# Top-k attention and a hard-swish feed-forward on one Trainium2 core: the reciprocals of the softmax move from VectorE to GpSimd, the shifts of exp from GpSimd to ScalarE

## The chip, the cores and the metric

One core of one Trainium2 chip runs the whole program. Its engines have instruction streams of their own and meet at semaphores: TensorE (PE in the profile; its weight loads are PEld), VectorE (DVE), ScalarE (ACT), GpSimd (POOL), and SyncE (SP), which here only issues DMAs. The metric is the device time of one execution in microseconds (us), the median of several runs; lower is better.

## The reference

```python
# q, k, v: (8 batches, 8 heads, 576 tokens, 64); top_k = 32
scores = scale * (q @ k.T)
kth = 32nd largest of each row
scores = where(scores >= kth, scores, -1e9)
scores = scores - max(scores)
attn = exp(scores); attn = attn / (sum(attn) + 1e-9)
x = (attn @ v) as (4608 tokens, 512)
h = x @ w_in                       # (4608, 2048)
g = h * clip(h + 3, 0, 6) / 6
out = g @ w_out                    # (4608, 512)
```

The two weight matrices arrive as float64. The kernel turns them into float32 itself, from the two 32-bit words of each number.

## The kernel before

The unit of attention work is a *duo*: two pairs of heads times one tile of 128 query rows, so four rows of 576 scores on each partition. The 64 tokens left over of each sequence (576 = 4 x 128 + 64) make smaller duos, here called rest duos, with two such rows. There are 64 full and 16 rest duos. For each row VectorE finds the 32 largest scores, by four MAX8 and three MATCH_REPLACE8. One duo is eight *slots*: in a slot VectorE does one MAX8 and one replacement on the two rows of a pair (one row in a rest duo), and every other step of the program is hung on a slot number. `u` is the pair in the duo, 0 or 1.

```python
def convert(dst, src):                     # one of 32 chunks of the weights, 128 x 512
    st = kqpool.tile(...); nc.sync.dma_start(st[:], src)
    yield
    a = gpool.tile(...); y = gpool.tile(...)
    nc.scalar.activation(a[:], hi.bitcast(F32), AF.Abs)
    nc.gpsimd.tensor_scalar(a[:], a[:], HI_MOST, HI_LEAST, ALU.min, ALU.max)
    nc.scalar.activation(y[:], lo, AF.Copy, bias=2.0, scale=2.0**-51)
    yield
    nc.vector.tensor_scalar(au, au, 3, None, ALU.logical_shift_left)              # L117
    nc.vector.scalar_tensor_tensor(out=yu, in0=hi, scalar=0x80000000, in1=yu, ...) # L118
    yield
    nc.gpsimd.tensor_tensor(dst.bitcast(I32), a.., y.., ALU.add)                  # L123

def shift(self, u):                                                # cut to its core
    nc.gpsimd.tensor_tensor(d[:, 0:nt], m[:, 0:nt, TOP_K - 1], m[:, 0:nt, 0], ALU.subtract)  # L263
    nc.gpsimd.tensor_scalar_mul(d[:, 0:nt], d[:, 0:nt], scale)                    # L266

def exp(self, u):
    for t in range(nt):  # row <- Prelu(kth - row): zero point at the 32nd largest   L273
        nc.scalar.activation(row, row, AF.Prelu, bias=m[:, t, TOP_K - 1 : TOP_K], ...)
    for t in range(nt):  # row <- exp(..), and its sum into den                      L278
        nc.scalar.activation(row, row, AF.Exp, bias=self.less[u][:, t : t + 1], ..., accum_out=self.den[:, u, t : t + 1])
    nc.scalar.activation(d, d, AF.Copy, bias=EPS)                                 # L283

def inverse(self, u):
    nc.vector.reciprocal(d, d)                                                    # L287

def weights(self, u):   # GpSimd: row * (1/den), then the float32 split in two halves of 16 bits
    ...                                                                           # L297, L306
def flip(self, u):      # DMA transpose of the 16-bit halves, on SyncE's queue
def join(self, u):      # the halves put together again: u = 0 on ScalarE, u = 1 on GpSimd  L318
def values(self, dst):  # TensorE: attn @ v into PSUM
def place(self):        # ScalarE: PSUM -> x, which queues a block of feed-forward
```

A feed-forward block (128 tokens) is cut into 16 *pieces* of matmul: 8 for `h`, 8 for `acc`. The main loop emits them between the steps of attention:

```python
due += ((left > 0) + (left >= 24) / 8 + (left >= 48) / 8) / (2 if u and u.rest else 1)
piece(int(due))         # left: pieces queued and not emitted
```

The slots of a duo's steps, counted from its own first slot:

```python
usual = dict(shift0=3, exp0=4, inverse0=9, weights0=10, flip0=12, join0=15,
             shift1=7, exp1=8, inverse1=13, weights1=14, flip1=16, join1=19, values=22, place=23)
behind = dict(usual, values=25, place=26)
early = dict(...)       # duos 0 and 1
soon = dict(..., values=16, place=17)   # the last two duos
```

`behind` holds for the duos from 10 to the fifth from the end.

## Time and profile before

| | |
|---|---|
| time, median of 3 runs | 1580.76 us (1580.28 to 1581.73) |
| profiled span | 1578.5 us |
| PE busy | 1456.9 us, 92% |
| DVE busy | 1466.8 us, 93% |
| ACT busy | 1096.3 us, 69% |
| POOL busy | 1144.5 us, 73% |
| mean granted TensorE clock | 0.963 |

Two engines are busy for more than nine tenths of the span, so neither share alone says which of them sets the time. The profile's rows by slice show VectorE at work from the start and idle in the last two of the 40 slices, and TensorE little used in the first five and at work to the end: work moves from the one to the other as the program runs. What matters is how the two are coupled in each stage.

### The profile page before, as it was taken

How to read it: one execution, taken by the hardware profiler on the slowest of the kernel's cores; microseconds unless marked ns; L12 is line 12 of the kernel's file. 1: busy time of each engine (PE TensorE's matmuls, PEld its weight loads, DVE VectorE, ACT ScalarE, POOL GpSimd, SP SyncE). 2: the span in 40 equal slices, each digit the busy share in tenths (PEclk: the TensorE clock that was granted, in tenths of full speed). 3: DMA queues.
4: the chain of work that ended last, by engine and by line, in shares of the span. 5: the costliest groups of instructions: out<-in, count | busy, mean ns of one | idle time of the engine just before them, and what ended most of it. 6: DMA issues, size and time to landing. Idle time of an engine off the chain costs nothing.

```text
span 1578.5 us, 28787 instructions
## 1 busy us (share of the span) xinstructions
PE 1456.9 (92%) x10272; PEld 1039.0 (66%) x10272; DVE 1466.8 (93%) x3105; ACT 1096.3 (69%) x1865; POOL 1144.5 (73%) x1264
## 2 busy tenths in 40 slices
PE   5256799979999999998999999999999999999899
PEld 3153566567767777666777777776777767677675
DVE  6999999999999999999999999999999999999700
ACT  6675777777777777777776786777766787777621
POOL 4868687777867777867687777867687777767841
PEclk9568999989999999999999999999999999999999
DMA  8652543444344543545254543446244443533410
GB/s 236 159 181 45 113 83 81 94 91 97 76 90 89 101 83 76 101 85 119 55 106 76 97 89 82 93 93 116 57 96 87 98 88 74 103 65 68 83 22 14
DMA packets 450319, 144.49 MB, mean 92 GB/s; under 512 B 433280, under 2 KB 441472, under 8 KB 450176
## 3 DMA queue, kind: packets, MB, share of 16 engines
q1 hardware_dynamic: 450176, 142.65, 43.5%
q8 instruction: 81, 1.33, 0.3%
q14 instruction: 62, 0.51, 0.1%
HBM read 45.09 MB, written 9.44 MB: 35 GB/s over the span
## 4 chain that ended last, share of the span: by engine, by line
DVE 51%; PE 35%; POOL 5%; issue 3%; ACT 3%; DMA 1%; SPq 1%; POOLq 0%; ACTq 0%; DVEq 0%
DVE m L250 26%; DVE wk L254 22%; PE h L365 14%; PE acc L385 13%; PE pv L338 4%; PE big L232 3%; POOL e L306 1%; DVE y L118 1%; POOL sc L297 1%; DMA t<-e 1%; POOL eT L318 1%; DVE a L117 1%; PE big L177 1%; ACT sc L278 1%; ACT eT L318 1%
## 5 line engine op out<-in xcount | busy, mean ns | idle before, releaser
L250 DVE MAX8 m<-wk 128x8 f32<-128x576 f32 x864 | 613.1, 746 | 2.2
L385 PE MATMUL acc<-w_out,g 128*128 128x512 f32 x1152 | 516.9, 600 | 14.1 <-POOL g L380 14.1
L365 PE MATMUL h<-xT,w_in 128*128 128x128 f32 x4096 | 485.5, 279 | 17.3 <-ACT xT L348 17.3
L365 PEld LDWEIGHTS h<-xT,w_in 128*128 128x128 f32 x4096 | 475.0, 195 | 39.5 <-issue 18.2
L254 DVE MATCH_REPLACE8 wk<-m,wk 128x576 f32<-128x576 f32 x576 | 423.7, 742 | 0.0
L385 PEld LDWEIGHTS acc<-w_out,g 128*128 128x128 f32 x1152 | 213.6, 191 | 260.4 <-issue 238.6
L297 POOL TENSOR_SCALAR sc<-sc,den 128x576 f32<-128x576 f32 x288 | 213.8, 753 | 229.9 <-DVE den L287 222.7
L306 POOL COPY e<-sc 128x2304 uint16<-128x2304 uint16 (+1 forms) x192 | 320.3, 1678 | 10.2
L278 ACT ACTIVATE sc<-sc,shift 128x576 f32<-128x576 f32 x288 | 220.4, 769 | 40.5 <-POOL shift L266 37.7
L318 ACT COPY eT<-t 128x2304 uint16<-128x2304 uint16 (+1 forms) x82 | 215.9, 2632 | 37.9 <-DMA t<-e 35.3
L273 ACT ACTIVATE sc<-sc,m 128x576 f32<-128x576 f32 x288 | 210.1, 777 | 46.2 <-DVE m L250 46.0
L338 PE MATMUL pv<-eT,vm 128*64 128x128 f32 (+1 forms) x2560 | 164.0, 273 | 57.9 <-ACT eT L318 45.8
L254 DVE MATCH_REPLACE8 wk<-m,sc 128x576 f32<-128x576 f32 x288 | 211.8, 742 | 0.0
L318 POOL COPY eT<-t 128x2304 uint16<-128x2304 uint16 (+1 forms) x78 | 203.8, 2613 | 6.9 <-DMA t<-e 6.5
L338 PEld LDWEIGHTS pv<-eT,vm 128*64 128x64 f32 x2560 | 135.2, 141 | 109.3 <-ACT eT L318 49.7
L250 DVE MAX8 m<-sc 128x8 f32<-128x576 f32 x288 | 203.3, 742 | 2.4 <-ACT sc L236 2.4
L373 ACT ACTIVATE g<-h,three 128x512 f32<-128x512 f32 x144 | 98.5, 684 | 150.0 <-PE h L365 140.6
L380 POOL TENSOR_TENSOR g<-g,hs 128x512 f32<-128x512 f32 x144 | 185.0, 1285 | 12.1 <-POOL g L379 0.2
L233 ACT COPY sc<-big 128x2048 f32<-128x2048 f32 (+1 forms) x65 | 119.3, 1836 | 26.1 <-PE big L232 26.0
L232 PE MATMUL big<-kq 64*128 64x512 f32 x512 | 136.4, 653 | 0.0
L379 POOL TENSOR_SCALAR g<-g 128x512 f32<-128x512 f32 x144 | 89.2, 620 | 62.6 <-ACT g L373 52.4
L395 ACT ACTIVATE o<-acc 128x512 f32<-128x512 f32 x36 | 21.4, 595 | 106.6 <-PE acc L385 106.6
(47 smaller groups left out, 1113.1 us busy)
## 6 DMA issues: line engine op xcount, KB each, us to landing
landed<-in_k_dram SPq DMA_DIRECT2D x64, 128.0 KB, 3.0
landed<-in_q_dram SPq DMA_DIRECT2D x64, 128.0 KB, 3.0
st<-in_moe_w_in_dram SPq DMA_DIRECT2D x16, 512.0 KB, 5.1
vm<-in_v_dram SPq DMA_DIRECT2D x64, 128.0 KB, 2.3
st<-in_moe_w_out_dram SPq DMA_DIRECT2D x16, 512.0 KB, 6.6
out_dram<-o SPq DMA_DIRECT2D x32, 256.0 KB, 2.4
t<-e SPq DMA_TRANSPOSE x160, 4.6
landed<-in_k_dram SPq DMA_DIRECT2D x32, 32.0 KB, 2.8
```

The lines of the kernel that those rows point to most:

```text
L232: nc.tensor.matmul(banks[:, 2 * i + hh, :], pr.qT[d, qs], pr.kT[d, :])
L250: nc.vector.max(self.m[u][:, t, 8 * r : 8 * r + 8], self.cur[t])
L254: nc.vector.match_replace(wk, self.m[u][:, t, 8 * r : 8 * r + 8], self.cur[t], LOWEST)
L273: nc.scalar.activation(row, row, AF.Prelu, bias=m[:, t, TOP_K - 1 : TOP_K], scale=-1.0, alpha=FLAT)
L278: nc.scalar.activation(row, row, AF.Exp, bias=self.less[u][:, t : t + 1], scale=-scale / FLAT, accum_out=self.den[:, u, t : t + 1],)
L297: nc.gpsimd.tensor_scalar(row, row, self.den[:, u, t : t + 1], 1.0, ALU.mult, ALU.mult)
L306: nc.gpsimd.tensor_copy(halves[:, :, to : to + c1 - c0], words)
L318: copy(eT[:, 0 : self.nb, :] .rearrange("p c q -> p (c q)") .bitcast(U16) .rearrange("p (x h) -> p h x", h=2), self.t16[u][:, 0 : 2 * self ...
L338: nc.tensor.matmul(pv[hh * D : (hh + 1) * D, u * w : (u + 1) * w], pr.vm[:, hh, c, :] if c < J else pr.vr[:, hh, :], rhs, start=(c == 0), ...
L365: nc.tensor.matmul(h[:, (f - f0) * P : (f - f0 + 1) * P], w_in[:, i, f * P : (f + 1) * P], xT[:, i, :], start=(i == 0), stop=(i == NHP - 1),)
L380: nc.gpsimd.tensor_tensor(g[:], g[:], hs[:], ALU.mult)
L385: nc.tensor.matmul(acc[:], gs[f // nf][:, f % nf * P : (f % nf + 1) * P], w_out[:, f, :], start=(f == 0), stop=(f == NFC - 1),)
```

## The change

Six things are changed together.

1. The reciprocal of the sums of exp leaves VectorE. GpSimd takes both pairs of a duo at once: x = den^(-1) as a power, then one Newton step x(2 - den x), four small instructions (`inverse`). Adding 1e-9 to the sums (`settle`) stays on ScalarE, once a duo. The first two duos and the last do it pair by pair.
2. The shift of exp leaves GpSimd: ScalarE works out scale x (kth - max) with one Copy and one Identity for each row.
3. For the first 16 of the 32 weight chunks, `y` is written to PSUM and `ys` takes VectorE's result in SBUF. The pool `g` goes from 8 to 7 buffers.
4. The first load of q is issued from ScalarE's queue, beside that of k on SyncE's.
5. Left-over tokens get two buffers in place of one (`xr`), and the rest duos of batch 2 are spread over the batch as in the later ones; in the last batch they come one query tile later.
6. The slots are set anew. From `exp` of pair 1 (slot 8) to `values` it is still 14 slots in `usual`. `soon` (values at 19) now holds for duos 2 to 9 and five near the end, `usual` for 10 to 29, `behind` from 30 to the ninth from the end.

The aim is to free VectorE, which paces the attention, of work that is not the search for the 32 largest.

```diff
--- before.py
+++ after.py
@@ -59,8 +59,8 @@
     wkpool = pool("wk", 1)
     mpool = pool("m", 4)
     xtpool = pool("xt", 3)
-    xrpool = pool("xr", 1)
-    gpool = pool("g", 8)
+    xrpool = pool("xr", 2)
+    gpool = pool("g", 7)
     hpool = pool("h", 2)
     opool = pool("o", 1)
     ps_big = pool("ps_big", 1, space=PSUM)
@@ -74,6 +74,8 @@
     make_identity(nc, ident[:])
     three = const([P, 1], "three")
     nc.vector.memset(three[:], 3.0)
+    minus = const([P, 2, 2], "minus")
+    nc.vector.memset(minus[:], -1.0)
     w_in = const([P, NHP, FF], "w_in")
     w_out = const([P, NFC, DM], "w_out")
@@ -93,7 +95,8 @@
     WC = 512
-    def convert(dst, src):
+    def convert(dst, src, early):
@@ -104,7 +107,11 @@
         words = st[:].rearrange("p (n two) -> p n two", two=2)
         lo, hi = words[:, :, 0], words[:, :, 1]
         a = gpool.tile([P, WC], F32, tag="g", name="a")
-        y = gpool.tile([P, WC], F32, tag="g", name="y")
+        y = (
+            ps_w.tile([P, WC], F32, tag="w", name="yp")
+            if early
+            else gpool.tile([P, WC], F32, tag="g", name="y")
+        )
         nc.scalar.activation(a[:], hi.bitcast(F32), AF.Abs)
         nc.gpsimd.tensor_scalar(a[:], a[:], HI_MOST, HI_LEAST, ALU.min, ALU.max)
@@ -113,15 +120,16 @@
+        ys = gpool.tile([P, WC], F32, tag="g", name="ys") if early else y
         au, yu = a[:].bitcast(U32), y[:].bitcast(U32)
         nc.vector.tensor_scalar(au, au, 3, None, ALU.logical_shift_left)
         nc.vector.scalar_tensor_tensor(
-            out=yu, in0=hi, scalar=0x80000000, in1=yu,
+            out=ys[:].bitcast(U32), in0=hi, scalar=0x80000000, in1=yu,
             op0=ALU.bitwise_and, op1=ALU.bitwise_or,
         )
         yield
         nc.gpsimd.tensor_tensor(
-            dst.bitcast(I32), a[:].bitcast(I32), y[:].bitcast(I32), ALU.add
+            dst.bitcast(I32), a[:].bitcast(I32), ys[:].bitcast(I32), ALU.add
         )
     def weight_chunks():
@@ -143,16 +151,17 @@
             self.b, self.hp = b, hp
             self.vm, self.vr, self.kr = vms[hp], vrs[hp], krs[b % 2 * NHP + hp]
-        def load(self):
+        def load(self, queue=None):
             h0 = 2 * self.hp
             t = self.landed = kqpool.tile([P, 2 * J + 1, 2, D], F32, tag="kq", name="landed")
-            for i, src in enumerate((k, q)):
+            for i, (src, eng) in enumerate(((k, nc.sync), (q, queue or nc.sync))):
                 for hh in range(2):
-                    nc.sync.dma_start(
+                    eng.dma_start(
                         t[:, i * J : (i + 1) * J, hh, :],
                         src[self.b, h0 + hh, 0:JP, :].rearrange("(p j) d -> p j d", j=J),
                     )
-                nc.sync.dma_start(
+                eng.dma_start(
                     t[i * R : (i + 1) * R, 2 * J, :, :],
                     src[self.b, h0 : h0 + 2, JP:S, :].rearrange("h s d -> s h d"),
                 )
@@ -259,11 +268,16 @@
         def shift(self, u):
             nt, m = self.nt, self.m[u]
-            d = self.less[u] = mpool.tile([P, 2], F32, tag="shift", name="shift")
-            nc.gpsimd.tensor_tensor(
-                d[:, 0:nt], m[:, 0:nt, TOP_K - 1], m[:, 0:nt, 0], ALU.subtract
-            )
-            nc.gpsimd.tensor_scalar_mul(d[:, 0:nt], d[:, 0:nt], scale)
+            d = self.less[u] = mpool.tile([P, 2, 2], F32, tag="shift", name="shift")
+            nc.scalar.activation(d[:, 1, 0:nt], m[:, 0:nt, 0], AF.Copy, scale=-scale)
+            for t in range(nt):
+                nc.scalar.activation(
+                    d[:, 0, t : t + 1],
+                    m[:, t, TOP_K - 1 : TOP_K],
+                    AF.Identity,
+                    bias=d[:, 1, t : t + 1],
+                    scale=scale,
+                )
         def exp(self, u):
@@ -276,15 +290,24 @@
             for t in range(nt):
                 row = self.row(u, t)
                 nc.scalar.activation(
-                    row, row, AF.Exp, bias=self.less[u][:, t : t + 1], scale=-scale / FLAT,
+                    row, row, AF.Exp, bias=self.less[u][:, 0, t : t + 1], scale=-scale / FLAT,
                     accum_out=self.den[:, u, t : t + 1],
                 )
-            d = self.den[:, u, 0:nt]
+        def inverse(self, us):
+            n, nt = len(us), self.nt
+            d = self.den[:, us[0] : us[-1] + 1, 0:nt]
+            x = mpool.tile([P, 2, 2], F32, tag="inv", name="inv")[:, 0:n, 0:nt]
+            y = mpool.tile([P, 2, 2], F32, tag="inv2", name="inv2")[:, 0:n, 0:nt]
+            nc.gpsimd.tensor_tensor(x, d, minus[:, 0:n, 0:nt], ALU.pow)
+            nc.gpsimd.tensor_tensor(y, d, x, ALU.mult)
+            nc.gpsimd.tensor_scalar(y, y, -1.0, 2.0, ALU.mult, ALU.add)
+            nc.gpsimd.tensor_tensor(d, x, y, ALU.mult)
+        def settle(self, us):
+            d = self.den[:, us[0] : us[-1] + 1, 0 : self.nt]
             nc.scalar.activation(d, d, AF.Copy, bias=EPS)
-        def inverse(self, u):
-            d = self.den[:, u, 0 : self.nt]
-            nc.vector.reciprocal(d, d)
         def weights(self, u):
@@ -408,9 +431,9 @@
             duos += [Duo(h, qt) for h in halves]
-            if qt == (0 if b == B - 1 else J - 1) and not 2 < b < B - 1:
+            if qt == (1 if b == B - 1 else J - 1) and not 1 < b < B - 1:
                 duos += [Duo(h, J) for h in halves]
-            elif 2 < b < B - 1 and qt % 2 == 0:
+            elif 1 < b < B - 1 and qt % 2 == 0:
                 duos.append(Duo(halves[qt // 2], J))
     assert J == NHP == 4
     per_batch = 2 * J + 2
@@ -418,7 +441,7 @@
     for u in duos[:2]:
         u.early = True
     todo = []
-    blocks = []
+    blocks, rests = [], []
     left = 0
     gates = []
@@ -442,8 +465,7 @@
     def queue(*block):
         nonlocal left
         todo.append(feed_forward(*block))
-        if block[0] is not state.get("xr"):
-            blocks.append(todo[-1])
+        (rests if block[0] is state.get("xr") else blocks).append(todo[-1])
         left += P // 8
     state = {}
@@ -454,7 +476,7 @@
         b, hp = u.pairs[0].b, u.pairs[0].hp
         if u.rest:
             if b % 2 == 0 and hp == 0:
-                while state.get("rest") in todo:
+                while len(rests) > 1 and rests[-2] in todo:
                     piece()
                 state["xr"] = xrpool.tile([P, NHP, P], F32, tag="xr", name="xr")
             u.values(state["xr"][:, hp : hp + 2, (b % 2) * R : (b % 2 + 1) * R])
@@ -478,7 +500,6 @@
                 for i in range(2)
             ]
             queue(state["xr"], rows)
-            state["rest"] = todo[-1]
     chunks = list(weight_chunks())
     landing, converting, adding = [], [], []
@@ -486,7 +507,7 @@
     def land(count=1):
         for _ in range(min(count, len(chunks))):
-            c = convert(*chunks.pop(0))
+            c = convert(*chunks.pop(0), early=len(chunks) >= NFC)
             next(c)
             landing.append(c)
@@ -513,7 +534,7 @@
         return pairs[b + 1][at - first] if b + 1 < B and 0 <= at - first < NHP else None
     first = pairs[0]
-    first[0].load()
+    first[0].load(nc.scalar)
     land(2)
     first[1].load()
     first[0].transpose()
@@ -530,33 +551,49 @@
     usual = dict(
-        shift0=3, exp0=4, inverse0=9, weights0=10, flip0=12, join0=15,
-        shift1=7, exp1=8, inverse1=13, weights1=14, flip1=16, join1=19, values=22, place=23,
+        shift0=3, exp0=4, shift1=7, exp1=8, settle01=8, inverse01=11, weights0=12, weights1=14,
+        flip0=14, flip1=16, join0=17, join1=19, values=22, place=23,
     )
     behind = dict(usual, values=25, place=26)
     early = dict(
-        shift0=3, exp0=3, inverse0=4, weights0=4, flip0=5, join0=8,
-        shift1=7, exp1=7, inverse1=8, weights1=8, flip1=9, join1=12, values=12, place=13,
+        shift0=3, exp0=3, settle0=3, inverse0=4, weights0=4, flip0=5, join0=8,
+        shift1=7, exp1=7, settle1=7, inverse1=8, weights1=8, flip1=9, join1=12, values=12, place=13,
     )
     soon = dict(
-        shift0=3, exp0=3, inverse0=5, weights0=5, flip0=7, join0=10,
-        shift1=7, exp1=7, inverse1=9, weights1=9, flip1=11, join1=14, values=16, place=17,
+        shift0=3, exp0=4, shift1=7, exp1=8, settle01=8, inverse01=9, weights0=9, weights1=11,
+        flip0=11, flip1=13, join0=14, join1=16, values=19, place=20,
+    )
+    last = dict(
+        shift0=3, exp0=3, settle0=3, inverse0=5, weights0=5, flip0=7, join0=10,
+        shift1=7, exp1=7, settle1=7, inverse1=8, weights1=8, flip1=9, join1=11, values=12, place=12,
     )
     queued = {}
     for m in range(ND):
-        for part, at in (early if m < 2 else soon if m >= ND - 2 else behind if per_batch <= m < ND - 4 else usual).items():
+        if m < 2:
+            when = early
+        elif m == ND - 1:
+            when = last
+        elif m < per_batch or m >= ND - 6:
+            when = soon
+        else:
+            when = behind if 3 * per_batch <= m < ND - 8 else usual
+        for part, at in when.items():
             queued.setdefault(8 * m + at, []).append((m, part))
     def parts(slot, late=None):
         for m, part in sorted(queued.get(slot, []), key=lambda x: x[1][:-1] != "shift"):
-            if late is not None and (part[:-1] in ("inverse", "weights")) != late:
+            if late is not None and (part[:7] in ("inverse", "weights")) != late:
                 continue
             if part == "values":
                 values(m)
             elif part == "place":
                 place(m)
+            elif part[:-1] in ("settle0", "inverse0"):
+                getattr(duos[m], part[:-2])((0, 1))
+            elif part[:-1] in ("settle", "inverse"):
+                getattr(duos[m], part[:-1])((int(part[-1]),))
             else:
                 getattr(duos[m], part[:-1])(int(part[-1]))
```

(Lines that are empty are cut.)

## The prediction

> **What bounds the kernel now.** I read the busy shares first, then busy time in stretches cut where the work changes, then VectorE's waits, then single instructions in the timeline. The page's first part:
>
> ```profile
> PE 1456.9 (92%) x10272; PEld 1039.0 (66%) x10272; DVE 1466.8 (93%) x3105; ACT 1096.3 (69%) x1865; POOL 1144.5 (73%) x1264
> ```
>
> Two engines are above nine tenths. The same by stretches (columns: stretch, its length, then busy us and instructions of PE, PEld, DVE, ACT, POOL; then granted clock, DMA share, GB/s); 13.6 is VectorE's first MAX8, 144.1 the first slot of duo 4, 708.6 that of duo 36, 1491.3 the end of the last MAX8:
>
> ```profile
> 708.60:1491.30 782.70, 774.06 (x5659) 556.66 (x5655) 777.35 (x1670) 570.25 (x974) 590.68 (x652) 1.00 0.44 87
> 1491.30:1578.50 87.20, 79.02 (x446) 54.92 (x444) 0.17 (x2) 19.30 (x33) 31.68 (x31) 0.98 0.10 23
> 244.20:708.60 464.40, 450.85 (x3243) 320.65 (x3243) 461.85 (x994) 339.94 (x578) 345.83 (x385) 0.98 0.45 89
> 13.60:144.10 130.50, 63.21 (x318) 43.04 (x318) 126.89 (x229) 89.50 (x148) 95.19 (x96) 0.71 0.54 160
> ```
>
> Up to 144 VectorE works nearly without a gap and TensorE half the time. In the middle both are at 97 to 99%. After 1491 VectorE has nothing left and TensorE needs 87 us for the backlog. So the span is VectorE's run of duos plus TensorE's tail. VectorE's own waits say who paces whom:
>
> ```profile
> DVE a L117 <- POOL a L109: 13.3, 2, 10.0
> DVE den L287 <- ACT den L283: 9.3, 4, 6.7
> DVE m L250 <- ACT sc L236: 2.4, 2, 1.7
> DVE three L76 <- PEq L616: 0.8, 1, 0.8
> ```
>
> 10.0 of the first line is the start and 6.7 of the second comes after the last MAX8, in the tail. Between, VectorE waits some 8 us in all. From the timeline's first MAX8 of each duo, a full duo takes 19.40 us and a rest duo 11.22, every time but two: duo 19 took 12.09 and duo 73 13.45, where a reciprocal waited for the sums. So VectorE is the pacemaker, but TensorE is close behind. I worked out what TensorE must do in one of the middle batches, with back-to-back times from the timeline: a block's 128 `h` records take 14.3 us and its 32 `acc` records 13.75, so one of 16 pieces is 1.75 us, and 4.5 blocks are 126 us; the scores of 8 full duos at 2.46 and 2 rest duos at 2.1 are 24; values, 8 at 2.33 and 2 at an estimated 1.5, are 22; four transposes at 1.15 are 4.5. Sum 176 us, against 8 x 19.40 + 2 x 11.22 = 177.6 of VectorE. TensorE has only 1.6 us a batch to spare.
>
> **What the Trainium skill says.** "SBUF — State Buffer", section "SBUF: two separate sides": VectorE and GpSimd share one pair of ports under an exclusive lock, taken by a VectorE instruction with two SBUF inputs or a two-port mode; the loser blocks. The trace agrees: L118, which reads `hi` and `y` from SBUF, takes 0.68 us free and 1.75 beside a GpSimd instruction. With `y` in PSUM it has one SBUF input. "ScalarE: Activation LUTs", section "What ACT_TABLE_LOAD costs": an ACTIVATE has about 186 ns fixed, 93 more for each per-partition operand, and neighbours overlap by about 93. The trace: the Copy of the sums takes 204 ns, and the instruction behind it starts 0.11 later. No page that I found states what a power costs on GpSimd; that number is missing from my sum.
>
> **The change part by part.**
>
> *The reciprocals.* The groups by shape (busy us, mean ns):
>
> ```profile
> L118 DVE SCALAR_TENSOR_TENSOR y<-st,y 128x512 uint32<-128x512 uint32 x32 | 30.2, 943 | 0.0
> L287 DVE RECIPROCAL den<-den 128x2 f32<-128x2 f32 x128 | 19.7, 154 | 7.2 <-ACT den L283 7.0
> ```
>
> 128 + 32 reciprocals are 24.6 us of busy time, but their busy time isn't what they cost. The timeline of VectorE, in a full and in a rest duo (start, duration):
>
> ```profile
> 187.78 0.73 DVE L254 MATCH_REPLACE8 wk<-m,wk 128x576 f32<-128x576 f32 x1
> 188.44 0.15 DVE L287 RECIPROCAL den<-den 128x2 f32<-128x2 f32 x1
> 188.51 0.73 DVE L250 MAX8 m<-wk 128x8 f32<-128x576 f32 x1
> ```
>
> ```profile
> 400.99 0.76 DVE L250 MAX8 m<-wk 128x8 f32<-128x576 f32 x1
> ...
> 401.86 0.74 DVE L254 MATCH_REPLACE8 wk<-m,wk 128x576 f32<-128x576 f32 x1
> 402.52 0.15 DVE L287 RECIPROCAL den<-den 128x2 f32<-128x2 f32 x1
> 402.64 0.76 DVE L250 MAX8 m<-wk 128x8 f32<-128x576 f32 x1
> ```
>
> From MATCH_REPLACE8 to MAX8 it is 0.73 us in a full duo, and 0.66 where no reciprocal stands between (190.61 to 191.27). So one costs 0.07 us of pace, 0.14 a duo. In a rest duo it is 0.78 with and without (400.21 to 400.99): the MAX8 there has to wait for the row just written, and the reciprocal fills that gap. Gain: 60 full duos after conversion x 0.14 = 8.4, the first four 0.6, and the stalls in duos 19 and 73 (0.87 + 2.23 = 3.1). Together 12.1 us, half of the busy time.
>
> *Conversion.* The first 16 L118 took 16.0 us by the timeline; at 0.68 each they would take 10.9. If PSUM removes the collisions: 5.1 us off VectorE's first 130 us, where nothing else bounds. The last 16 stay.
>
> *The first load.* The transposes of k start at 4.54, those of q at 6.67, after q's load, which SyncE issued from 2.82 on. Issued beside k's from 0.7 on, q should land 1.8 us sooner, and everything to the first MAX8 hangs on it. Gain 1.8.
>
> *Shifts.* GpSimd loses 160 x (0.22 + 0.22) = 69 us and gains 83 inverses of four small instructions: three at 0.22 and a power that I put at 0.3 to 0.6, so 80 to 105 us. GpSimd stays near 74%. ScalarE gains three small ACTIVATEs for a full pair, two for a rest pair: with ends overlapped I put 0.55 and 0.35 us, 128 x 0.55 + 32 x 0.35 = 82 us, and loses 77 of 160 additions (16 us): up 66 us to some 74%. Its waits for GpSimd's shift (37.7 us, 26 times) go. None of this is on VectorE's path, as long as ScalarE's copies of scores come in time.
>
> *Slots.* Stepping through the emission rule, I counted the pieces put out by each duo. The new table puts batch 0's blocks three slots earlier, so TensorE is three pieces ahead up to duo 29, but from duo 36 (224 pieces out in both) to duo 71 both kernels emit the same number at every duo. At the end of VectorE's work 534 of 576 pieces are out before, 535 after: the tail is one piece shorter, 1.75 us. The blocks begin at slot 21 in both. TensorE's wait of 4.4 us for a `join` on GpSimd at 1491, when `values` of duo 77 came due, should shrink, as these last duos now follow `soon`; I count 3.
>
> *Sum.* 12.1 + 5.1 + 1.8 + 1.75 + 3 = 23.8 us. From this I take back: of VectorE's 7.1 us gained after duo 36 (35 full duos x 0.14, and 2.2) TensorE can follow only in part, since it idles 8.6 us there in all and its work of 176 us meets a pace of 176.5 (8 x 19.26 + 2 x 11.22): 3 us go into a longer tail. And 2 us for new stalls: at duos 10, 20, 30, 68 and 74, all right after a rest duo, the scores were copied only 0.4 to 1.9 us before VectorE needed them, and ScalarE gets about 1 us more to do there. Net 19: 1580.8 - 19 = 1562; I predict 1561.
>
> **Rivals.** *TensorE is the bound already.* For it: the chain that ended last runs on TensorE from 733 to 1220, and the busy share is 98.9% after duo 36. Then only what comes before TensorE fills up counts (start and conversion, 7 us), and the time is about 1573. Against it: VectorE's period is 19.40 to a hundredth, so TensorE never held it up, and at 1491 TensorE had caught up and was waiting. *ScalarE or GpSimd takes the place.* If the power takes 3 us in place of 0.5, GpSimd rises by 200 us to over 85%, chains run past their slots, TensorE, which takes its work in order, stops at `values`, and the scores behind it come late: 1590 to 1620. For it: the four rest-duo edges with under 1 us of slack, and the fact that a Newton step is needed at all, which speaks for a coarse and thus perhaps short routine. Against it: GpSimd idles 27%, 222.7 us of it waiting for the very reciprocal it now makes itself. *All of it arrives,* the rest-duo stalls too, and TensorE closes its idle time: 1550.
>
> **Range and chances.** The sure parts (reciprocals in the first half, start, most of conversion) are 10 us, the full sum 24, and the GpSimd rival costs some tens. Range 1547 to 1578. Faster by over 2% means under 1549.1, more than my whole sum before deductions: 0.08. Slower by over 2% (over 1612) needs the slow power: 0.04.
>
> **What would show it.** Full duos at 19.26 between first MAX8s, rest duos still at 11.22; duo 4 begins near 136.5; first MAX8 near 11.8; the first 16 of VectorE's second conversion instruction at 0.7 each; VectorE's last MAX8 near 1472 to 1475 and a tail of 83 to 87 us behind it. I am wrong if the power takes over 1 us, if VectorE waits for scores at many duo edges, or if the tail grows by what VectorE gains.

## The result, and the profile after

The changed kernel takes 1624.13 us (median of 4 runs, 1623.21 to 1625.23), the kernel before 1581.24 in the same session: a ratio of 1.0269, 95% interval 1.0251 to 1.0287. It is slower by 43 us. The prediction, 1561, had the wrong sign.

Busy shares of the changed kernel, first part of its page:

```profile
PE 1470.6 (91%) x10272; PEld 1043.4 (64%) x10272; DVE 1456.2 (90%) x2946; ACT 1161.7 (72%) x2236; POOL 1199.5 (74%) x1276
```

The loads are as the change intends: VectorE 10.6 us less, ScalarE 65.4 more (predicted 66), GpSimd 55 more. TensorE does the same 10272 matmuls in 13.7 us more, at a mean granted clock of 0.955 instead of 0.963. No engine comes near its span but the two that did before. So the 43 us can't be read off the busy shares. The chain of work that ended last shows a different picture from before, when VectorE held 51% and TensorE 35% of it (before, then after):

```profile
DVE 51%; PE 35%; POOL 5%; issue 3%; ACT 3%; DMA 1%; SPq 1%; POOLq 0%; ACTq 0%; DVEq 0%
PE 57%; POOL 15%; DVE 14%; DMA 5%; ACT 4%; issue 3%; SPq 2%; POOLq 0%; ACTq 0%
```

The same by stretches (length, busy us of PE, PEld, DVE, ACT, POOL, then clock, DMA share, GB/s); 13.4 is the first MAX8, 154.5 the first slot of duo 4, 258.0 that of duo 10, 733.2 that of duo 36; the last MAX8 ends at 1518.6:

```profile
13.40:154.50 141.10, 64.29 (x319) 42.34 (x320) 124.16 (x223) 89.51 (x165) 97.01 (x106) 0.73 0.53 155
258.00:733.20 475.20, 452.18 (x3186) 318.42 (x3187) 459.49 (x941) 356.57 (x696) 362.23 (x385) 0.97 0.43 86
733.20:1518.50 785.30, 771.33 (x5597) 552.66 (x5596) 772.57 (x1581) 604.99 (x1170) 615.26 (x645) 0.99 0.45 86
1518.50:1621.40 102.90, 88.75 (x510) 62.13 (x508) 0.11 (x1) 24.77 (x42) 42.62 (x44) 0.93 0.16 31
```

The three boundaries give an account of the whole:

| | before | after | difference |
|---|---|---|---|
| duo 4 starts | 144.1 | 154.5 | +10.4 |
| from there to the end of the last MAX8 | 1347.2 | 1364.1 | +16.9 |
| tail behind the last MAX8 | 87.2 | 102.8 | +15.6 |
| span | 1578.5 | 1621.4 | +42.9 |

Every stage has become longer, the middle one too, where VectorE has less to do. There, the timeline's first MAX8 of each duo shows a full duo at 19.28 us instead of 19.40, so 60 of them gain 7.2 us. But the 16 rest duos took 206.8 us together instead of 182.4: nine of them took over 12 us, up to 17.2, where 11.22 had been the rule. VectorE's waits name what happens there (us in total, times, longest):

```profile
DVE m L259 <- ACT sc L245: 27.6, 11, 5.9
DVE a L125 <- POOL a L116: 16.6, 4, 9.8
DVE y L126 <- ACT y L118: 7.0, 2, 4.7
DVE ys L126 <- POOL w_in L131: 3.2, 1, 3.2
```

The first line was 2.4 us before: VectorE waits for the copied scores of the next duo. The other three are conversion. The timeline of VectorE at the end of rest duo 62 shows such a wait, of 3.46 us, ahead of duo 63 (start, duration, in brackets the idle time ahead):

```profile
1206.01 0.74 DVE L263 MATCH_REPLACE8 wk<-m,wk 128x576 f32<-128x576 f32 x1
1206.79 0.76 DVE L259 MAX8 m<-wk 128x8 f32<-128x576 f32 x1
1211.01 1.42 DVE L259 MAX8 m<-sc 128x8 f32<-128x576 f32 x2 [3.46 <-ACT sc L245]
```

And the timelines of TensorE and ScalarE in the same place:

```profile
1197.36 7.31 PE L388 MATMUL h<-xr,w_in 128*128 128x128 f32 x64
1204.51 0.61 PE L235 MATMUL big<-kr,kq 128*128 128x128 f32 x4
1205.05 1.99 PE L241 MATMUL big<-kq 64*128 64x512 f32 x8
1207.86 0.76 ACT L292 ACTIVATE sc<-sc,shift 128x576 f32<-128x576 f32 x1
1208.75 0.20 ACT L310 ACTIVATE den<-den 128x4 f32<-128x4 f32 x1
1208.86 1.85 ACT L242 COPY sc<-big 128x2048 f32<-128x2048 f32 x1
1210.61 0.38 ACT L245 COPY sc<-big 128x256 f32<-128x256 f32 x1
```

The matmuls of the scores start at 1204.5, after pieces of feed-forward that TensorE had been ordered to do first, and end at 1207.0; the copy starts 1.8 us after that, because ScalarE is still at the exp of the pair before. A rest duo lasts 11 us where a full one lasts 19, but scores need almost as much of TensorE, so if TensorE is late, this is where it shows.

It is not TensorE alone, though. From duo 4 on, eleven waits for copied scores make up 26.5 us, each at the end of a rest duo. At five of them (9.3 us) the copy starts within 0.4 us of the end of the matmuls, so the matmuls were late. At five others (11.4 us) ScalarE was busy with older work for 0.9 to 6.0 us in between, and at one (5.9 us) the copy started 3.2 us after the matmuls, when GpSimd had finished with `e`, which it makes from such rows.

The costs of the moved operations by shape (busy us, mean ns, then idle time ahead):

```profile
L303 POOL TENSOR_TENSOR inv<-den,minus 128x4 f32<-128x4 f32 x61 | 62.9, 1031 | 11.1 <-ACT den L310 11.0
L303 POOL TENSOR_TENSOR inv<-den,minus 128x2 f32<-128x2 f32 x22 | 15.7, 711 | 0.0
L304 POOL TENSOR_TENSOR inv<-den,inv 128x4 f32<-128x4 f32 x61 | 12.7, 208 | 4.8
```

```profile
L274 ACT ACTIVATE shift<-m,shift 128x1 f32<-128x1 f32 x288 | 71.7, 288 | 22.6 <-DVE m L259 17.7
L272 ACT ACTIVATE shift<-m 128x2 f32<-128x2 f32 x128 | 27.2, 213 | 0.1
```

```profile
L126 DVE SCALAR_TENSOR_TENSOR y<-st,y 128x512 uint32<-128x512 uint32 x16 | 19.2, 1203 | 7.0 <-ACT y L118 7.0
L126 DVE SCALAR_TENSOR_TENSOR ys<-st,yp 128x512 uint32<-128x512 uint32 x16 | 10.8, 674 | 3.2 <-POOL w_in L131 3.2
```

A power of four elements a partition takes 1.03 us, five times a product of the same shape. The shifts of a full pair are one instruction of 0.213 and two of 0.288 us on ScalarE; their ends overlap with their neighbours', and ScalarE's busy time as a whole rose by 65.4 us. With `y` in PSUM VectorE's instruction takes 674 ns, 16 times.

### The profile page after: what moved, and what is told of

It reads as the page before. It is cut to its first block, busy times and chain, and to the rows that moved or that the text cites. A ratio compares the mean times of both kernels' runs of the same rounds, so it can differ in the third digit from the quotient of the medians.

```text
span 1621.4 us, 28967 instructions
## 1 busy us (share of the span) xinstructions
PE 1470.6 (91%) x10272; PEld 1043.4 (64%) x10272; DVE 1456.2 (90%) x2946; ACT 1161.7 (72%) x2236; POOL 1199.5 (74%) x1276
## 4 chain that ended last, share of the span: by engine, by line
PE 57%; POOL 15%; DVE 14%; DMA 5%; ACT 4%; issue 3%; SPq 2%; POOLq 0%; ACTq 0%
PE h L388 22%; PE acc L408 21%; DVE m L259 7%; PE pv L361 6%; DVE wk L263 6%; PE big L241 4%; POOL e L329 4%; DMA t<-e 4%; POOL sc L320 3%; POOL eT L341 3%; POOL g L403 1%; POOL inv L303 1%; PE big L186 1%; PE big L224 1%; PE big L235 1%
## 5 line engine op out<-in xcount | busy, mean ns | idle before, releaser
L408 PE MATMUL acc<-w_out,g 128*128 128x512 f32 x1152 | 526.6, 607 | 16.4 <-POOL g L403 16.4
L341 POOL COPY eT<-t 128x2304 uint16<-128x2304 uint16 (+1 forms) x78 | 203.7, 2612 | 167.9 <-DMA t<-e 164.3
L361 PE MATMUL pv<-eT,vm 128*64 128x128 f32 (+1 forms) x2560 | 167.8, 277 | 89.0 <-ACT eT L341 39.0
L259 DVE MAX8 m<-sc 128x8 f32<-128x576 f32 x288 | 203.5, 744 | 28.2 <-ACT sc L245 27.6
L341 ACT COPY eT<-t 128x2304 uint16<-128x2304 uint16 (+1 forms) x82 | 215.9, 2633 | 17.5 <-DMA t<-e 14.8
L398 ACT COPY hs<-h 128x512 f32<-128x512 f32 x144 | 83.3, 578 | 7.7 <-POOL g L403 7.7
```

Of the source, the lines that this page charges most:

```text
L259: nc.vector.max(self.m[u][:, t, 8 * r : 8 * r + 8], self.cur[t])
L341: copy(eT[:, 0 : self.nb, :] .rearrange("p c q -> p (c q)") .bitcast(U16) .rearrange("p (x h) -> p h x", h=2), self.t16[u][:, 0 : 2 * self ...
L361: nc.tensor.matmul(pv[hh * D : (hh + 1) * D, u * w : (u + 1) * w], pr.vm[:, hh, c, :] if c < J else pr.vr[:, hh, :], rhs, start=(c == 0), ...
L408: nc.tensor.matmul(acc[:], gs[f // nf][:, f % nf * P : (f % nf + 1) * P], w_out[:, f, :], start=(f == 0), stop=(f == NFC - 1),)
```

## The experiments

Eighteen kernels were run in five rounds. The recorded texts give theories letters. In my words: **A** says that the order of the steps on GpSimd is the trouble (the duo-wide inverse and the joins that wait for the DMA transposes); **G**, formed late, says that TensorE is already full, so that anything that makes it wait, on whichever engine, is lost time, at the rest duos and in the tail. The letters between stand for single parts of the change: the work added to GpSimd, the work added to ScalarE, conversion, slots and places. Each text says which it means.

### First round: the order on GpSimd

```diff
# e1_slots_back: the changed kernel with pair 0's old slots
-    settle01=8, inverse01=11, weights0=12, flip0=14, join0=17
+    settle01=8, inverse01=9, weights0=10, flip0=12, join0=15
# e2_pair_by_pair: the changed kernel, power pair by pair in the old slots (usual and soon)
-    settle01=8, inverse01=11, ...
+    settle0=4, inverse0=9, weights0=10, ..., settle1=8, inverse1=13, ...
# e3_fused_vector: the changed kernel, one reciprocal a duo on VectorE
-    power and Newton step on GpSimd
+    nc.vector.reciprocal(d, d)
# e4_conversion: the kernel before with point 3 of the change alone (y in PSUM, g 7)
```

> The changed kernel, with only the slots of pair 0 in the usual table as they were: inverse at 9 (was 11), weights 10 (12), flip 12 (14), join 15 (17). The inverse stays fused and on GpSimd. Theory A (order: in the changed kernel the join of the duo before stands ahead of inverse and both weights in GpSimd's order, so its wait for the DMA transpose holds everything up): GpSimd's wait of 164 us for transposes falls under 60 us, the rest duos come back to about 11.3 us, and the time to 1585 to 1600 (what is left is conversion, some 10 us, and a part of the tail). Theory B (the power's own 1.03 us and the three small instructions after it fill GpSimd): still 1615 or more. Theory C (ScalarE's added shifts make the scores late): still 1615 or more, with rest duos at 13 to 15 us.

> The changed kernel, with the inverse on GpSimd but pair by pair, and all slots of the usual table as in the kernel before; soon is pair by pair too. Twice as many powers. Theory A: 1585 to 1600, like the run with only the slots of pair 0 put back, since pair 0's weights again go ahead of the join. Theory B: slower than the changed kernel or the same, 1620 to 1640, as GpSimd has about 60 us more to do. Theory C: 1615 or more.

> The changed kernel, with its slots and the fused inverse, but made by one reciprocal on VectorE. No power, no Newton step. Theory A: nearly as slow as the changed kernel, 1605 to 1622, since the order on GpSimd is the same; the wait for transposes stays over 100 us. Theory B: back to 1570 to 1590. Theory C: 1615 or more.

> The kernel before, with only the changed conversion of weights (y of the first 16 chunks in PSUM) and 7 in place of 8 buffers of g. If conversion itself caused the 10.4 us by which duo 4 begins later in the changed kernel: 1588 to 1593, duo 4 near 154. If the 10 us came from the power and the shifts standing among the conversions: 1572 to 1580, with duo 4 near 139 to 142 as I predicted.

| | us | ratio to before (95%) | duo 4 | rest duos, sum | tail |
|---|---|---|---|---|---|
| e1_slots_back | 1644.20 | 1.0397 (1.0379 to 1.0414) | 155.7 | 225.1 | 99.0 |
| e2_pair_by_pair | 1617.59 | 1.0240 (1.0222 to 1.0257) | 154.3 | 207.6 | 96.5 |
| e3_fused_vector | 1615.12 | 1.0215 (1.0200 to 1.0230) | 148.5 | 206.1 | 88.4 |
| e4_conversion | 1583.07 | 1.0010 (1.0003 to 1.0016) | 146.0 | 183.3 | 87.2 |

(Duo 4 is its start. Rest duos and tails are worked out from each kernel's timeline.)

The changed kernel's GpSimd waits 164.3 us for transposes in front of its joins, before only 6.5. That was the natural suspect (before, then after):

```profile
POOL eT L318 <- DMA t<-e: 6.5, 3, 4.9
POOL eT L341 <- DMA t<-e: 164.3, 53, 10.2
```

GpSimd's waits in e1:

```profile
POOL inv L303 <- ACT den L310: 218.6, 58, 12.4
POOL eT L341 <- DMA t<-e: 19.5, 10, 4.8
```

The old slots take the wait for the transposes nearly away, and the kernel becomes slower by 20 us: now GpSimd stands at the inverse, at slot 9, until ScalarE has finished the sums of pair 1, which it begins at slot 8. A wait only changed its name; the slots of the change were right for a duo-wide inverse. e2, without the duo-wide inverse, gains 6.5 us of 43. Theory A falls as the main cause. e3 gains 9 us with everything else left as it was, and its start improves by 6 us, so the power has a part. But VectorE has its own trouble there, waiting for sums at 17 places, and GpSimd's joins wait as before:

```profile
DVE den L301 <- ACT den L305: 35.6, 17, 4.3
```

```profile
POOL eT L336 <- DMA t<-e: 171.2, 49, 12.9
```

So e3 isn't a clean undoing. Conversion alone (e4) costs 1.8 us instead of gaining 5.

### Second round: one part alone

```diff
# f1_shift_gpsimd: the changed kernel with the shifts back on GpSimd
# f2_shift_scalar: the kernel before with the shifts on ScalarE
# f3_power_only: the kernel before, pair by pair and in its own slots, with
-    nc.vector.reciprocal(d, d)
+    pow(d, -1), then x(2 - den x), on GpSimd
# f4_layout_only: the kernel before with xr 2, g 7, the new places of rest duos and the
# new ranges of the slot tables; the reciprocal on VectorE pair by pair (soon: inverse0=6, inverse1=10)
```

> The changed kernel, with the shifts of exp back on GpSimd (a subtraction and a multiplication a pair); all else as changed. Theory C (ScalarE's added shifts make the scores late at the edges of rest duos): rest duos back to 11.3 us, 1585 to 1597. Theory D (the new slots, rest places and buffers): 1615 to 1630, as now or slower. Theory B (the power on GpSimd): slower than now, since GpSimd gets 69 us more: 1630 or more.

> The kernel before, with only the shifts of exp moved to ScalarE as in the changed kernel. Theory C: slower by 20 to 35 us, 1600 to 1616, with rest duos at 12 to 15 us. Theories B and D: 1575 to 1585.

> The kernel before, with only the reciprocals made on GpSimd, pair by pair, as a power and a Newton step; slots as before. Theory B: slower by 20 us or more, 1600 or more. Theories C and D: within 8 us of before, and VectorE's full duos at 19.26 to 19.28.

> The kernel before, with only the changed layout: two buffers for left-over tokens and 7 for g, the rest duos' new places, soon (values at slot 19) for duos 2 to 9 and five near the end, a last duo of its own, behind from duo 30. The reciprocals stay on VectorE and the shifts on GpSimd, pair by pair. Theory D: slower by 20 us or more, 1600 or more. Theories B and C: 1572 to 1588.

| | us | ratio to before (95%) | duo 4 | rest duos, sum | tail |
|---|---|---|---|---|---|
| f1_shift_gpsimd | 1630.98 | 1.0315 (1.0298 to 1.0332) | 154.2 | 214.0 | 103.6 |
| f2_shift_scalar | 1593.55 | 1.0083 (1.0068 to 1.0098) | 143.9 | 194.5 | 87.1 |
| f3_power_only | 1591.22 | 1.0067 (1.0052 to 1.0082) | 150.9 | 191.0 | 90.2 |
| f4_layout_only | 1612.03 | 1.0197 (1.0182 to 1.0212) | 152.4 | 199.1 | 89.3 |

No part alone is free. Shifts on ScalarE cost about 13 us, nearly all at the rest duos (194.5 against 182.4), while start and tail stay. But in f2 VectorE still makes the reciprocals, and it is at these that it waits, for sums that ScalarE finishes later; its waits for scores stay at 2.3 us:

```profile
DVE den L292 <- ACT den L288: 18.8, 10, 4.1
```

Before, this wait is 9.3 us. So f2 shows a way that the changed kernel no longer has, and isn't the price of the shifts there; the third round gives that. The power costs about 10.6 even in the old slots, 6.8 of it before duo 4, although its full duos run at 19.28 as hoped. f2 and f3 both lie between the times that the texts gave for and against their part. f1 says that the shifts would be worse still, by 7 us, on GpSimd once the power is there.

f4 looks like the largest part, but it has a fault of its own. VectorE's reciprocals in my pair-by-pair table come too soon for the sums:

```profile
DVE den L287 <- ACT den L283: 31.3, 11, 9.5
```

Up to 22 us (31.3 less the 9.3 of before) of f4's 31 are therefore a trouble that the change doesn't have. f4 doesn't measure the layout, and nothing below rests on it.

### Third round: leaving work out

```diff
# g1_no_inverse: the changed kernel; weights aren't divided by the sums
-    the four instructions of inverse
+    pass
# g2_no_inverse_no_shift: the same; and exp is taken without its shift (bias 0)
# g3_before_no_inverse: the kernel before without its reciprocals on VectorE
# g4_before_no_inverse_g7: the kernel before
-    gpool = pool("g", 8)
+    gpool = pool("g", 7)
```

> The changed kernel, leaving out the inverse (no power, no Newton step, on no engine; the rows are multiplied by the sums themselves), with all else as changed. Theory E (the loads: what the power costs on GpSimd and the shifts on ScalarE each lengthen the chain that ends in the copy of the scores at the edges of rest duos, and the conversions): faster than the changed kernel by 18 to 32 us, 1592 to 1606, duo 4 near 147, tail near 90. Theory F (the new slots, rest places and buffers by themselves): at most 10 us faster, 1614 or more.

> The changed kernel, leaving out both the inverse and the shifts of exp (exp gets a zero as its bias): what is left of the change is the slots, the rest places, the buffers and the conversion, with VectorE freed. Theory E: rest duos back to 11.3 us, 1570 to 1588. Theory F: 1600 or more, rest duos still at 12 to 15 us.

> The kernel before, leaving out only the reciprocals: what a VectorE freed of them is worth by itself, with no load on another engine. My step of 12.1 us holds and TensorE follows: 1566 to 1571. TensorE is the bound: 1575 to 1581.

> The kernel before, leaving out the reciprocals, and with 7 in place of 8 buffers of g. If the missing buffer is what lengthened duo 3 in the run with the changed conversion alone (39.3 us against 33.8): duo 3 at 38 to 41 us and 4 to 7 us slower than the same kernel with 8. If the conversion's PSUM tiles did it: duo 3 at 33 to 35 us and the same time.

By an oversight the kernel of the last label kept its reciprocals, contrary to its name and recorded text. It is the kernel before with seven buffers `g` and nothing else, and is to be compared with the kernel before.

| | us | ratio to before (95%) | duo 4 | rest duos, sum | tail |
|---|---|---|---|---|---|
| g1_no_inverse | 1606.05 | 1.0150 (1.0135 to 1.0165) | 148.8 | 202.4 | 95.2 |
| g2_no_inverse_no_shift | 1585.59 | 1.0031 (1.0019 to 1.0043) | 145.3 | 189.2 | 95.0 |
| g3_before_no_inverse | 1573.70 | 0.9949 (0.9934 to 0.9964) | 144.2 | 188.3 | 83.2 |
| g4_before_no_inverse_g7 | 1587.47 | 1.0037 (1.0023 to 1.0052) | 150.2 | 184.2 | 87.9 |

g3 shows the most that freeing VectorE of its reciprocals can bring in the kernel before: 0.5%, about 8 us. And not in the way I thought. Its full duos run at 19.28 too, yet the last MAX8 ends 1.5 us sooner than before; the rest duos give back 5.9 of the gain, waiting for scores, and 4 us come out of the tail:

```profile
DVE m L250 <- ACT sc L236: 10.0, 5, 3.1
```

Before this wait was 2.4. Duos 19 and 73 still take 13.0 and 14.2 us, so their stalls, which I had put down to late reciprocals, need none. VectorE couldn't run ahead by even 8 us in 1347: something else sets its speed. That is where theory G comes from.

The steps from g3 to the changed kernel add up: from g3 to g2 11.9 us, to g1 20.5, to the changed kernel 18.1. So the inverse on GpSimd costs about 18 us (with 129 us of GpSimd's time). The shifts on ScalarE cost 20.5 here as a whole, not against their old place. The 11.9 us between g3 and g2 are conversion, slots and places; since g3 still has shifts on GpSimd and g2 none anywhere, 11.9 is the least they can be put at if taking the shifts off GpSimd does no harm; the tail alone differs by 11.8.

g2 closes the case of theory A. Its GpSimd waits for the transposes as long as ever, and yet most of what its rest duos had grown by is gone (189.2 in sum, four of them still over 12 us), and the run from duo 4 to the last MAX8 is back at 1346.4 us:

```profile
POOL eT L324 <- DMA t<-e: 175.8, 51, 12.1
```

g4 settles conversion. One `g` buffer less costs 0.37%, about 6 us, all before duo 4 (150.2 instead of 144.1). In e4, which also has `y` in PSUM, it is 1.8, so PSUM gives some 4 us, and the missing buffer takes 6.

### Fourth round: a lighter TensorE

```diff
# k1_before_half_acc (of the kernel before), k2_after_half_acc (of the changed kernel):
# every second matmul of acc is left out, so half of the sum over the hidden layer is missing
+            if f % 2 == 0:
                 nc.tensor.matmul(acc[:], ..., start=(f == 0),
-                    stop=(f == NFC - 1))
+                    stop=(f == NFC - 2))
# i1_last_values: the changed kernel, table of the last duo
-    join1=11, values=12, place=12
+    join1=14, values=16, place=17
# h1_psum_y_q_queue: the kernel before with y in PSUM for 16 chunks, g still 8,
# and the first q on ScalarE's queue
```

> The kernel before, leaving out every second matmul of the second feed-forward product (acc over the even chunks of the hidden layer alone): TensorE has about 248 us less to do, no other engine less. It is the base for the same cut in the changed kernel. VectorE's run should stay: last MAX8 near 1488, rest duos at 11.2 us; the tail loses some 20 us, so 1553 to 1562.

> The changed kernel, leaving out the same half of the second product. Theory G (TensorE is full; each delay of what it waits for is lost time, and VectorE pays for it at the edges of rest duos): with TensorE relieved the rest duos come back to 11.2 to 11.5 us in spite of the same loads on GpSimd and ScalarE, last MAX8 near 1495, and the time is within 12 us of the kernel before with the same cut. Theory H (GpSimd's and ScalarE's own chains are too long for a rest duo, whatever TensorE does): rest duos stay at 12 to 15 us and the time is 25 to 43 us over the kernel before with the same cut.

> The changed kernel, with the last duo's values at slot 16 (was 12), place 17 and join 14, as late as in the kernel before: more feed-forward pieces stand ahead of the last values in TensorE's order. If the tail of 103 us comes from TensorE standing at the last values for GpSimd's join (10.4 us there): tail 92 to 97, 1613 to 1618. If from elsewhere: the same as changed within 3 us.

> The kernel before with the two parts of the change that cost no other engine anything: y of the first 16 chunks in PSUM, with 8 buffers of g kept, and the first load of q on ScalarE's queue. From the runs: 5.9 us lost by 7 buffers and 1.8 by both together leave a gain of 4.1 for PSUM. Expected 1573 to 1578; no gain if the two do not add up.

| | us | ratio to before (95%) | duo 4 | rest duos, sum | tail |
|---|---|---|---|---|---|
| k1_before_half_acc | 1556.55 | 0.9847 (0.9833 to 0.9860) | 143.3 | 179.2 | 67.6 |
| k2_after_half_acc | 1572.78 | 0.9951 (0.9937 to 0.9964) | 154.8 | 181.3 | 77.1 |
| i1_last_values | 1614.23 | 1.0211 (1.0195 to 1.0226) | 156.5 | 204.3 | 93.8 |
| h1_psum_y_q_queue | 1576.81 | 0.9976 (0.9966 to 0.9985) | 139.9 | 183.0 | 87.2 |

This pair decides between G and H. k2 has all the loads of the change on GpSimd and ScalarE, the power, the shifts, the slots, and only TensorE has less to do. Its stretches from duo 4 to the last MAX8, and behind it, columns as above; then the same two of k1:

```profile
154.80:1493.40 1338.60, 1151.50 (x8960) 877.20 (x8961) 1330.03 (x2721) 1042.34 (x2026) 1061.76 (x1115) 0.93 0.45 88
1493.40:1570.50 77.10, 61.97 (x414) 47.01 (x412) 0.00 (x1) 22.96 (x37) 35.80 (x39) 0.90 0.15 32
143.30:1487.40 1344.10, 1148.80 (x8946) 863.03 (x8947) 1338.48 (x2874) 984.61 (x1677) 1012.02 (x1120) 0.94 0.45 89
1487.40:1555.00 67.60, 61.22 (x428) 48.16 (x427) 0.19 (x2) 19.31 (x33) 31.67 (x31) 0.97 0.13 30
```

TensorE is busy 86% of the first stretch, ScalarE and GpSimd as long as in the changed kernel (1042 and 1062 us, there 1042 and 1057). Fifteen of the 16 rest duos take 11.2 us again; the other, duo 9, 13.3. VectorE's wait for scores has gone from 27.6 us to

```profile
DVE m L259 <- ACT sc L245: 3.7, 2, 2.0
```

while GpSimd still waits for its transposes:

```profile
POOL eT L341 <- DMA t<-e: 149.3, 53, 6.4
```

With room on TensorE the run from duo 4 to the last MAX8 is 1338.6 us, shorter than k1's 1344.1 by 5.5. That is about the gain that the change was made for: 60 full duos x 0.12 = 7.2, less the 2.1 of duo 9. What remains of the change's loss, k2 against k1 by span, is 15.5 us: +11.5 up to duo 4, -5.5, +9.5 in the tail. The start is as bad here as in the full kernels (+10.4 there), and of the 15.6 us lost in the tail 9.5 stay: these two don't come from a full TensorE. For the same reason the time misses theory G's 12 us: by medians k2 is 16.2 over k1. Nor is TensorE the whole of the middle stage: g2, with TensorE as full as ever but without the inverse and the shifts, runs it in 1346.4. The loss there needs both, the added work and a TensorE without room. And where ScalarE itself is late, room on TensorE doesn't help: ahead of duo 10, the one wait of k2 in this stage (2.0 us), the copy starts 6.4 us after the matmuls, 6.0 of them with ScalarE at work.

i1 gives back 9.9 us with one table. The changed kernel asks for `values` of the last duo at slot 12, one slot behind the join of pair 1. TensorE takes its work in order, so pieces queued behind it stand still. TensorE's wait for GpSimd's joins in the tail, changed kernel and then i1:

```profile
PE pv L361 <- POOL eT L341: 10.4, 2, 6.5
```

```profile
PE pv L361 <- POOL eT L341: 3.8, 1, 3.8
```

h1 takes from the change `y` in PSUM and the load of q, with all 8 buffers, and is 0.24% under the kernel before. VectorE's instruction in its conversion takes 674 ns where `y` is in PSUM, and 918 in the other half, for which the changed kernel needed 1203:

```profile
L123 DVE SCALAR_TENSOR_TENSOR ys<-st,yp 128x512 uint32<-128x512 uint32 x16 | 10.8, 674 | 0.0
L123 DVE SCALAR_TENSOR_TENSOR y<-st,y 128x512 uint32<-128x512 uint32 x16 | 14.7, 918 | 0.0
```

Its 4 us are won before duo 4 (139.9 instead of 144.1) and stay to the end: the last MAX8 ends at 1487.8 instead of 1491.3, and the tail is the same.

### Last round

```diff
# i2_product_for_power: the changed kernel; the first operation of inverse is a product,
# so the quotient is not computed and the chain has the same length without a power
-    nc.gpsimd.tensor_tensor(x, d, minus, ALU.pow)
+    nc.gpsimd.tensor_tensor(x, d, minus, ALU.mult)
# h2_feed_earlier: h1, and TensorE gets values sooner, from duo 2 on
+    ahead = dict(usual, values=21, place=22)     # duos 2 to 9; usual 10 to 29, behind from 30
```

> The changed kernel, leaving out the power: a product of the same two operands stands in its place (so no reciprocal is made), the three small instructions after it stay. The power is 78.6 of the 129 us that the inverse takes on GpSimd, and leaving out the whole inverse gained 18.1 us. If GpSimd's time is what counts: a gain of 9 to 13 us, 1611 to 1615. If the number of steps in the chain counts more than their length: under 5 us, 1619 or more.

> The kernel with y of the first 16 chunks in PSUM and the first q on ScalarE's queue (the run before), and with values of duos 2 to 9 one slot earlier (21) and those of duos 10 to 29 at 22 in place of 25, as in the changed kernel. If TensorE is the bound, getting its work earlier gains 2 to 5 us more: 1571 to 1575. If not, the same or slower: 1576 to 1580.

i2: 1610.91 us, 1.0187 (1.0172 to 1.0203). Of the 18.1 us that the inverse costs, 13.2 go when the power is a product and three other small operations stay. The power's own duration is thus most of it. A product at some 0.2 us takes 17 us in all where the power took 78.6, so 62 us less of GpSimd's time are worth 13 us to the program, a fifth.

h2: 1578.89 us, 0.9985 (0.9979 to 0.9992): no gain over h1 (0.9976), if anything a loss of 1 to 2 us. By its recorded text this speaks against TensorE as the bound of that kernel: there, with the reciprocals on VectorE and the shifts on GpSimd, getting its work sooner is worth nothing. Rest duos 8, 9 and 28 take 12.0 to 12.5 us each, because VectorE waits at its reciprocals for sums (0.8 to 1.3 us), not for scores.

## Why the prediction was wrong

**Right.** Full duos at 19.26: they take 19.28. ScalarE's load: 65 us more, predicted 66. The instruction with `y` in PSUM at 0.7: 674 ns at each of 16. "SBUF — State Buffer", section "SBUF: two separate sides", has it that VectorE takes the ports it shares with GpSimd for an instruction in a two-port mode, and for one with two SBUF inputs when GpSimd reads SBUF too; with `y` in PSUM one SBUF input is left, and in h1 all 16 took 670 to 679 ns, 12 of them while GpSimd was at work. The shift on ScalarE: I put 0.55 us with ends overlapped; "ScalarE: Activation LUTs", section "What ACT_TABLE_LOAD costs", gives 186 + 93 ns for one with a per-partition operand, and the trace has 288.

**The step that failed** is the path. Of ScalarE's new work I wrote "None of this is on VectorE's path, as long as ScalarE's copies of scores come in time", and I took GpSimd's to be covered, since it "idles 27%". For all moved work together I took back 2 us of new stalls. It costs 38.5 us: leaving out the inverse gives back 18.1 (g1), leaving out the shifts as well another 20.5 (g2; that is all that the shifts cost, not the difference to their old place, which no run gives cleanly). The copies don't come in time. VectorE's waits for them rise from 2.4 to 27.6 us, and of the eleven from duo 4 on six have ScalarE or GpSimd at older work in front of the copy.

Behind it stands the choice against the first rival, *TensorE is the bound already*. I rejected it because "VectorE's period is 19.40 to a hundredth, so TensorE never held it up". The observation is true, but it doesn't show how much room TensorE has left, only that VectorE found its scores ready at that pace. My own sum gave 1.6 us of room a batch, 1%, and I should have believed it. g3 shows that even with nothing added anywhere, 6 us of VectorE's gain are lost at once as waits at rest duos. There, too, ScalarE stands between: at the four waits for scores from duo 4 on its copy starts 2.8 to 5.7 us after the matmuls. The k pair shows what room on TensorE is worth: 27 of the 43 us (42.9 less 15.5) go with it, under the same load on the other engines, because scores are then ready early enough to cover what comes after them (in k2 a copy starts as late as 10.0 us after its matmuls without VectorE waiting). The other 15.5 stay, and lie in the start and the tail. The rival by itself wasn't right either: it gave 1573, since it too counted the moved work as free.

**Sizes.** *The power*: I put it at 0.3 to 0.6 us, and wrote that I am wrong if it takes over 1: it takes 1.03 for four elements, 0.71 for two. The inverse as a whole took 129 us of GpSimd (78.6 of power and 50.5 of the three others, from the groups) in place of 80 to 105. The rival *ScalarE or GpSimd takes the place* had the time, 1590 to 1620, nearly right, but by luck in part: it needed a power of 3 us, the power of 1.03 has a third of that, and the rest came from elsewhere. *The reciprocals' gain* of 12.1 us: g3 gives about 8, and the 3.1 us of it for duos 19 and 73 never came.

*Conversion*: gain of 5.1 us predicted. I computed it for the instruction and overlooked the pool: a chunk takes two buffers of `g` as before (`a`, and `ys` or `y`), but `g` had been cut from 8 to 7. Duo 3 took 40.9 us instead of 33.8, ScalarE waiting with `y` for GpSimd to be done with an older chunk (17.5 us, where 2.5 before). g4 puts the missing buffer alone at 6 us. Duo 4 began at 154.5, not at 136.5: 6 of the 10.4 us lost belong to `g`, less the 4 gained by PSUM, and 5.7 to the inverse and 3.5 to the shifts (g1 and g2, by their duo 4); these sum to 11.2, so within about a microsecond.

*The first load*: gain of 1.8 us predicted for the first MAX8; it came at 13.4 instead of 13.59. In the changed kernel the transposes of k start at 5.63 instead of 4.54, and those of q follow them at 6.51 instead of 6.67: with q's load beside it, k's came later, and of the 1.8 us 0.2 were left.

*The tail*: predicted 83 to 87, one piece shorter. It is 102.8. I counted the pieces that are put out, not how far TensorE has come with them: at the end of the last MAX8 it has 510 matmuls left, where 446 before, and is busy for 9.7 us more. The other 6.0 us it stands idle (14.2 in the tail, before 8.2, in i1 8.3): the table `last` makes it wait, in front of everything queued, and i1, which changes that table alone, takes 9 us of the tail away (93.8). I had expected TensorE's wait of 4.4 us there to shrink; it rose to 10.4.

**Open.** Why ScalarE comes late to the copies, by its own load or by what it waited for earlier, isn't told apart. Which of TensorE's many short waits carries how much of the middle stage isn't told apart: in the changed kernel they are spread over the transposed x from ScalarE, joins of both engines and PSUM, each a few us. That matmuls took 13.7 us longer at a lower granted clock goes together with more idle time; whether the one causes the other wasn't tried. The layout of rest duos and the two buffers for them were never measured cleanly (f4), so of the 11.9 us or more of the smaller parts only the pool `g`, `y` in PSUM and the table `last` have a number of their own. Single profiles of kernels that agree up to a point differ there by up to 2 us (duo 4 at 154.5 and at 156.5 in i1, which is the same program up to its end), so differences of that size between stages aren't read.

## What to carry to other kernels

Here two engines were busy for 97 to 99% of a stretch. Taking work off one of them brought no more than about 8 us of the 12 hoped for (g3), and work moved onto engines that idled more than a quarter of the time was paid with 38.5: it delays what the full engines take from them. Measure the second engine's room directly, by taking work from it in a run (half of its matmuls, say), before believing that it follows. Keep chains that feed an in-order engine far enough ahead of it, take a pool's buffers into the sum (one of eight was worth 6 us here), and change one table at a time.

## What the runs showed that I had not expected

- A power on GpSimd takes 1031 ns for 128 x 4 elements and 711 ns for 128 x 2, in f3 576 for 128 x 1; the other small operations of the inverse take 189 to 227. Each further element of a partition adds 135 to 160 ns.
- A reciprocal of 154 ns between two dependent instructions of VectorE costs 0.06 of pace a time (19.40 against 19.28 a full duo, two of them each), and nothing in a rest duo, where it fits a gap.
- Leaving out half of the matmuls of `acc` takes 181 us off TensorE's busy time (1456.9 to 1276.0), not the 258 that half of 516.9 would be: those that stay take 646 ns each instead of 600, at a mean granted clock of 0.919 instead of 0.963. The time of the kernel before falls by 24 us, of which 20 are the tail (87.2 to 67.6): from duo 4 to the last MAX8 VectorE, at 1344.1 instead of 1347.2, sets the pace there even with room on TensorE.
